# Zero products in TensorE's planned waits, a pattern's spread moved to GpSimd's queue, later keys, and new due times

## The chip, the cores and the metric

The kernel runs on one core of a Trainium2 chip. The metric is device time in microseconds of that core; the time before is the median of three runs. A profile is one more execution, recorded instruction by instruction. The engines are TensorE (PE; its weight loads are listed as PEld), VectorE (DVE), ScalarE (ACT), GpSimd (POOL) and SyncE (SP), each with its own queue, which it works through in order.

## The reference

Four sequences, eight heads, 768 positions, 64 dimensions per head. Attention looks at six chunks of 32 keys per query, chosen by an upper bound on the chunk's scores, and its result goes through a gated feed-forward network with 512 inputs and 1536 hidden units:

```
k_min, k_max = min, max of k over each chunk of 32 keys
ub     = sum(max(q * k_min, q * k_max))            # per query and chunk
ub     = ub where the chunk is not behind the query, else -1e9
sel    = the 6 chunks with the largest ub
scores = q @ k.T / 8, -1e9 outside sel and behind the query
x      = softmax(scores) @ v                       # heads side by side: 3072 x 512
out    = (sigmoid(x @ w_gate) * (x @ w_val)) @ w_out
```

## The kernel before

The work is cut into nine stages: the first sequence in three (128, 256 and 384 queries), each further sequence in two halves of 384. A stage has three parts. `prep` brings keys and queries with the head dimension on partitions (`kTp`, `qT` in the first three stages, transposes on VectorE later), takes minimum and maximum per chunk (`kxn`, `kcat`), multiplies the bounds out (`m_ub`, L969), compares with the sixth largest and puts the result as 25 more rows under the queries in `headQ` (L997). Stage zero has so few chunks that nothing is selected; it has a guard instead (`first_guard`, `m_ub` at L936). `attn` makes scores (`big_sc` or `m_sc`, L1046) against `headK`, whose 25 rows at partition 64 hold the patterns that turn the 25 rows of `headQ` into a mask, then the exponential (`at`, L1051), the diagonal's mask on GpSimd (L1057), the product with the values (`m_pv`, L1071), the division (`xnat`) and the transpose (`m_xtp`, L1096). `ffn` makes `m_g` and `m_v` (L1125), the gate (L1134), `hglu` (L1136) and `m_o` (L1146), and stores it.

Nothing is written in the order in which it runs. Each piece is a task in `Plan`, with a priority (a due time plus entries of the table `NUDGE`), one or several engines with a duration each, the keys that it reads and writes, and its tiles. `order` puts the tasks on the engines with those durations, and the program is emitted in the order of the planned starts. So the table and the constants decide the order on each engine; on the chip the engines wait for each other by semaphores alone. Tasks on the lanes `Q0` and `Q2` are empty: they stand for a transfer's landing in the plan and emit nothing. `WLAND` holds the planned landings of the nine thirds of weights (`weight_tasks`: w0 to w5 are `wg` and `wv` in turn, w6 to w8 are `wo`, all issued by GpSimd), and `LOADS` those of the first sequence's keys, queries, values and pattern spreads on SP's and ScalarE's queues.

A spread (`_spread`, L646) copies the 25 rows of a pattern, made by `_pattern` on GpSimd for one head, to the other heads by a DMA. The spread for the first half (`p00`) goes by SP's queue. The loads of the next sequences' keys and queries (`_blocks`, L661) go by SP's queue too, and so do the stores of `out` (L1161). `fill` (L581) emits products of zeros into a bank of PSUM; the plan calls it only ahead of TensorE's first task.

Of the kernel before, what the change touches and what calls it, by code (L numbers as in the profile page):

```python
# [8 lines left out]
F32 = mybir.dt.float32  # L9
F16 = mybir.dt.float16  # L10
# [12 lines left out]
    "#c.0": 0.4, "#c.1": -7.8, "wst0": -58.5, "#wst0.0": -1.1, "w0": -26.5, "#w0.0": 2.5, "#c.2": -0.1, "wst1": -42.4,  # L23
    "#wst1.0": 77.9, "w1": 59.5, "#w1.0": -28.8, "#c.3": -8.7, "#c.4": -30.2, "v": 61.3, "#v.0": 12.6, "wst2": 4.3,
    "#wst2.0": -73.1, "w2": -9.6, "#w2.0": 2.9, "#c.5": 6.6, "#c.6": 6.2, "wst3": -12.3, "#wst3.0": -1.3, "w3": 31.2,
    "wst4": 0.2, "#wst4.0": 0.2, "w4": -1.7, "#w4.0": -30.1, "wst5": 20.7, "#wst5.0": 62.1, "w5": 1.3, "#w5.0": -16.3,
    "wst6": 2.6, "#wst6.0": 63.7, "w6": 34.0, "#w6.0": 26.2, "wst7": -36.4, "#wst7.0": -22.5, "w7": -9.8,
    "wst8": -28.7, "#wst8.0": 184.1, "w8": -13.6, "#w8.0": 15.0, "#c.7": 28.2, "#c.8": 65.6, "kch": 94.9,
    "#kch.0": 10.3, "is": -163.2, "qch": 120.2, "#qch.0": 3.5, "vn": -29.4, "#vn.0": -16.8, "#is.1": -44.3,
    "#vn.1": -1.6, "#kch.1": -9.0, "#qch.1": 11.7, "#kch.2": -19.3, "#qch.2": 5.6, "#is.2": 25.2, "#vn.2": -8.5,  # L30
    "#c.9": 7.3, "#vn.3": -9.2, "#v.1": -1.9, "#v.2": 0.6, "#v.3": 9.4, "kTp0": -37.9, "prep:0": -5.0,
    "#kTp:0.0": -4.5, "kxn0": -126.7, "#kxn:0.0": -41.0, "#kxn:0.1": -0.4, "#kc:0.0": 45.4, "hk0": 1.5,
    "#hk:0.0": 3.0, "#hk:0.1": 16.0, "#hk:0.2": 6.0, "#hk:0.3": 0.8, "qT0": 3.8, "#qT:0.0": 4.6, "Qc0": -121.7,
    "#Qc:0.0": 7.2, "#Qc:0.1": -14.0, "#Qc:0.2": -5.2, "#Qc:0.3": -1.9, "ubp0": -30.8, "#ubp:0.0": -23.3,
    "#ubp:0.1": 19.4, "#c.10": -30.9, "#c.11": -6.7, "gT0": -4.3, "#gT:0.0": -23.1, "#gT:0.1": 6.5, "#c.12": -9.9,
    "Ap0": 10.2, "#Ap:0.0": -3.8, "#Ap:0.1": -11.3, "#c.13": -18.6, "v0": 6.8, "load:0": 54.9, "#v:0.0": 11.2,
    "#v:0.1": -90.7, "sc0": -12.2, "attn:0": -38.0, "#sc:0.0": 1.4, "at0": -27.1, "#at:0.0": -7.4, "#at:0.1": -37.4,
    "pv0": -22.8, "#pv:0.0": 63.4, "#pv:0.1": -10.0, "#pv:0.2": -4.6, "#pv:0.3": 23.2, "xn0": -12.6, "#xn:0.0": 33.2,
    "xtp0": -31.4, "#xtp:0.0": -7.3, "xT0": 59.7, "#xT:0.0": 56.1, "#sc:0.1": 25.2, "#at:0.2": 37.5, "#at:0.3": 10.0,
    "#pv:0.4": -20.9, "#pv:0.5": -1.7, "#pv:0.6": -62.7, "#pv:0.7": 25.8, "#xn:0.1": 30.1, "#xtp:0.1": -0.4,  # L40
    "#xT:0.1": 4.2, "#kch.3": 69.9, "#qch.3": -9.0, "#kch.4": 25.8, "#qch.4": 3.2, "#kch.5": -3.5, "#qch.5": -0.9,
    "#c.15": 2.7, "#vn.4": -3.2, "#v.4": -23.4, "#vn.5": 23.4, "#v.5": 72.9, "#vn.6": 26.6, "#v.6": -22.5, "gv0": 0.4,
    "ffn:0": 2.1, "#gv:0.0": -31.3, "#gv:0.1": -14.7, "#gv:0.2": 17.1, "#gv:0.3": -12.2, "#gv:0.4": 45.7,
    "#gv:0.5": 1.8, "#gate:0.0": -21.5, "hglu0": 21.2, "#hglu:0.0": 60.4, "#gv:0.6": -2.4, "#gv:0.7": 46.8,
    "#gv:0.8": 3.1, "#gv:0.10": -11.2, "#gate:0.1": -22.7, "#hglu:0.1": -27.8, "#gv:0.12": -16.4, "#gv:0.13": -20.6,
    "#gv:0.14": -7.9, "#gv:0.15": 5.9, "#gv:0.16": 28.2, "#gv:0.17": 20.7, "#gate:0.2": 7.7, "#hglu:0.2": -0.4,
    "#gv:0.18": 20.0, "#gv:0.19": 1.6, "#gv:0.20": -8.1, "#gv:0.21": 10.7, "#gv:0.22": 41.9, "#gv:0.23": 8.8,
    "#gate:0.3": -5.2, "#hglu:0.3": 12.5, "o0": 0.6, "#o:0.0": 20.6, "#o:0.1": -8.9, "#o:0.2": 17.4, "#o:0.3": 56.4,
    "#o:0.4": 13.4, "#o:0.5": -24.0, "#osb:0.0": -16.7, "out0": 17.0, "kTp1": 6.5, "prep:1": -1.7, "#kTp:1.0": -2.1,
    "kxn1": 37.4, "#kxn:1.0": -46.3, "#kxn:1.1": 7.9, "#kTp:1.1": 11.8, "#kxn:1.2": 27.8, "kc1": 0.1, "#kc:1.0": 24.9,  # L50
    "hk1": 41.1, "#hk:1.0": -36.9, "#hk:1.1": 18.5, "#hk:1.2": -11.6, "#hk:1.3": 30.2, "qT1": -33.9, "#qT:1.0": -31.0,
    "Qc1": 103.7, "#Qc:1.0": 26.5, "#Qc:1.1": -10.1, "#Qc:1.2": -10.3, "#Qc:1.3": 12.8, "#qT:1.1": 15.6,
    "#Qc:1.4": 5.7, "#Qc:1.5": -21.6, "#Qc:1.6": -18.7, "#Qc:1.7": -21.2, "#hq:1.0": -10.7, "#hq:1.1": -0.6,
    "ub1": -2.1, "ubq1": -27.3, "#ubq:1.0": -21.1, "#ubq:1.1": 47.9, "mx81": -5.0, "#mx8:1.0": -48.4, "Ap1": 4.8,
    "#Ap:1.0": 15.8, "apT1": -41.3, "#apT:1.0": 20.4, "mq1": 2.4, "#mq:1.0": 3.4, "#mq:1.1": -18.2, "#mq:1.2": 25.8,
    "#mq:1.3": 25.9, "#ub:1.1": 27.0, "#ubq:1.2": 9.4, "#ubq:1.3": 2.8, "#mx8:1.1": 26.0, "#Ap:1.1": 26.7,
    "#apT:1.1": 4.0, "#mq:1.5": 24.9, "#mq:1.6": 2.4, "#mq:1.7": -39.3, "sc1": 1.4, "attn:1": -238.2, "#sc:1.0": -6.4,
# [1173 lines left out]
```

## Time and profile before

| | us |
|---|---|
| median of three runs | 304.28 (304.17 to 304.63) |
| the profiled execution | 305.13 |
| its span, first to last instruction | 303.3 |
| TensorE busy | 285.6 |
| VectorE busy | 213.6 |
| ScalarE busy | 196.4 |
| GpSimd busy | 111.2 |

The mean granted clock of TensorE is 0.960 of full. The page cuts the span into 40 slices and gives the busy tenths of each engine and the granted clock; groups of instructions follow by line and tile, with their count, busy time and mean, and the idle time ahead of them with what ended it. In rows in order of time the first number is the start, the second the duration (of all instructions of the row), then the engine, the line, the operation and its tiles. A wait is put down to what came last. A matmul's end is modelled, so the pace of a row of matmuls is better read from the start of the next one.

### The profile page before, as it was taken

The page shows a single profiled execution, that of the slowest core. Times are in us where ns is not written, and L with a number is a line of the kernel's source. Part 1 is how long each engine was busy: PE and PEld are TensorE (multiplying, and loading weights), DVE is VectorE, ACT ScalarE, POOL GpSimd, SP SyncE. Part 2 cuts the span into 40 slices and gives each one's busy share as a digit, 9 for nine tenths or more (in the row PEclk, how much of TensorE's full clock was granted, in tenths as well). Part 3 has the DMA queues.
Part 4 walks back from the last instruction along what each step waited for, and adds up shares of the span by engine and source line. Part 5 has one row for each costly group of instructions (what it writes and reads, how often), then busy time and mean ns, then how long its engine had stood idle before and what let it go on. Part 6 is the DMA issues. An engine that isn't in the chain of part 4 may idle for free.

```text
span 303.3 us, 6733 instructions
## 1 busy us (share of the span) xinstructions
PE 285.6 (94%) x2594; PEld 183.1 (60%) x2594; DVE 213.6 (70%) x585; ACT 196.4 (65%) x292; POOL 111.2 (37%) x176
## 2 busy tenths in 40 slices
PE   7466999999999999999999999999999999999994
PEld 3344995776566556665656566676656666655551
DVE  3677289899999899989998995898667234221322
ACT  2685789699496589578965667599644825622322
POOL 7944711286667243117941242058312001200000
PEclk9657599999999999999999999999999999999999
DMA  7999999999999570511970100018000000120102
GB/s 153 267 212 268 230 173 106 169 159 158 167 163 176 108 161 4 87 19 40 182 93 1 50 21 3 0 37 85 5 2 35 37 0 2 37 104 0 71 0 104
DMA packets 110004, 27.98 MB, mean 92 GB/s; under 512 B 100207, under 2 KB 105365, under 8 KB 109973
## 3 DMA queue, kind: packets, MB, share of 16 engines
q1 hardware_dynamic: 81669, 19.43, 31.7%
q0 software_dynamic: 26592, 7.47, 24.5%
q10 hardware_dynamic: 1712, 0.66, 0.9%
q8 instruction: 20, 0.33, 0.4%
q14 instruction: 11, 0.09, 0.1%
HBM read 28.31 MB, written 6.29 MB: 114 GB/s over the span
## 4 chain that ended last, share of the span: by engine, by line
PE 81%; DMA 7%; DVE 5%; POOL 2%; ACT 1%; issue 1%; SPq 0%; POOLq 0%; DVEq 0%; ACTq 0%
PE m_o L1146 18%; PE m_v L1125 17%; PE m_g L1125 16%; PE big_sc L1046 12%; PE m_pv L1071 7%; DMA ld_v<-in_v_dram 6%; PE big_gv L1125 5%; PE m_ub L969 4%; PE m_xtp L1096 2%; DMA ld_qb<-in_q_dram 1%; DVE Qcat L909 1%; DVE kxn L809 1%; DVE kT_kT L878 1%; DVE hglu L1136 0%; DVE Qcat L765 0%
## 5 line engine op out<-in xcount | busy, mean ns | idle before, releaser
L1051 ACT ACTIVATE at<-big_sc 128x896 f16<-128x896 f32 (+3 forms) x96 | 84.0, 908 | 21.1 <-PE big_sc L1046 19.1
L1146 PE MATMUL m_o<-wo,hglu 128*128 128x512 f16 x288 | 73.6, 379 | 0.0
L1125 PE MATMUL m_g<-xT,wg 128*128 128x384 f16 (+2 forms) x384 | 69.0, 312 | 1.4 <-ACT xT L1100 1.4
L1125 PE MATMUL m_v<-xT,wv 128*128 128x384 f16 (+2 forms) x384 | 69.2, 310 | 0.2 <-DVE hglu L1136 0.2
L1136 DVE SCALAR_TENSOR_TENSOR hglu<-gate,m_v 128x384 f16<-128x384 f16 (+1 forms) x88 | 45.5, 531 | 29.7 <-PE m_v L1125 23.9
L1057 POOL TENSOR_SCALAR_AFFINE_SELECT at<-at 128x384 f16<-128x384 f16 (+2 forms) x66 | 34.8, 531 | 85.7 <-ACT at L1051 81.8
L1134 ACT ACTIVATE gate<-m_g 128x384 f16<-128x384 f32 (+1 forms) x88 | 39.9, 475 | 29.5 <-PE m_g L1125 18.4
L1125 PEld LDWEIGHTS <-wg 128*128 128x128 f16 x432 | 41.0, 101 | 23.5 <-issue 2.8
L1125 PEld LDWEIGHTS <-wv 128*128 128x128 f16 x432 | 40.2, 100 | 22.9 <-issue 1.9
L1046 PE MATMUL big_sc<-headQ,headK 89*128 89x128 f16 (+2 forms) x472 | 51.0, 246 | 2.7 <-ACT headQ L997 1.8
L1046 PEld LDWEIGHTS <-headK 89*128 89x128 f16 x472 | 34.1, 99 | 15.6 <-issue 4.8
L1146 PEld LDWEIGHTS <-hglu 128*128 128x128 f16 x288 | 25.6, 97 | 21.6 <-issue 1.2
L1071 PEld LDWEIGHTS <-at 128*128 128x128 f16 x672 | 30.5, 100 | 12.3 <-issue 3.1
L1071 PE MATMUL m_pv<-v,at 128*128 128x65 f16 x672 | 34.9, 196 | 0.0
L997 POOL COPY headQ<-apT 25x384 f16<-25x384 f16 (+1 forms) x33 | 16.2, 491 | 36.4 <-DVE apT L993 35.3
L909 DVE STREAM_TRANSPOSE Qcat<-ld_qb 64x768 f32<-64x768 f32 x24 | 23.1, 967 | 0.4
L776 POOL CAST headQ<-Qcat 64x1536 f16<-64x1536 f32 (+1 forms) x11 | 15.6, 1420 | 20.9 <-ACT Qcat L761 10.9
L1136 DVE SCALAR_TENSOR_TENSOR hglu<-gate,big_gv 128x384 f16<-128x384 f16 x12 | 6.5, 552 | 18.2 <-ACT gate L1134 7.8
L1083 DVE TENSOR_TENSOR xnat<-m_pv,rz 128x384 f16<-128x384 f32 (+1 forms) x34 | 18.2, 534 | 1.2
L1153 ACT ACTIVATE osb<-m_o 128x512 f32<-128x512 f32 x16 | 9.5, 597 | 12.5 <-PE m_o L1146 12.2
L1134 ACT ACTIVATE gate<-big_gv 128x384 f16<-128x384 f32 x12 | 5.8, 490 | 17.9 <-PE big_gv L1125 17.3
L680 POOL DMA_DIRECT2D v<-in_v_dram x18 | 16.3, 922 | 0.5 <-PE m_pv L1071 0.5
(109 smaller groups left out, 301.0 us busy)
## 6 DMA issues: line engine op xcount, KB each, us to landing
out_dram<-osb SPq DMA_DIRECT2D x24, 256.0 KB, 2.0
ld_kb<-in_k_dram SPq DMA_DIRECT2D x24, 192.0 KB, 3.5
ld_qb<-in_q_dram SPq DMA_DIRECT2D x24, 192.0 KB, 4.0
v<-in_v_dram POOLq DMA_DIRECT2D x21, 128.0 KB, 7.3
ld_k<-in_k_dram SPq DMA_DIRECT2D x6, 256.0 KB, 14.2
wg<-in_moe_w_gate_dram POOLq DMA_DIRECT2D x3, 512.0 KB, 15.1
wv<-in_moe_w_val_dram POOLq DMA_DIRECT2D x3, 512.0 KB, 15.4
wo<-in_moe_w_out_dram POOLq DMA_DIRECT2D x3, 512.0 KB, 30.2
```

The source lines that it names most:

```text
L680: nc.gpsimd.dma_start(dst[:, :, i, :], v[b, :, r0 + 128 * i:r0 + 128 * i + 128].rearrange("h p d -> p h d"))
L909: nc.vector.transpose(tl(qd, [128, H, HS])[0:64, h:h + 2].rearrange("p a (c t) -> p a c t", t=CH), tl(("ld", "qb", b, u))[64 * e:64 * e + ...
L997: copy(tl(("headQ", s), [89, H, st.n], F16)[64:89, h, :], tl(apT)[32 * i:32 * i + 25, :])
L1046: nc.tensor.matmul(ps[:, 128 * o:128 * (o + m)], (hk if s else firstK)[0:rows, h, jl:jl + 128], (tl(("headQ", s)) if s else first)[0:rows, ...
L1051: add(at(x + 0.03 * t + 0.01), [("ACT", 0.19 + w * 0.815e-3, lambda sc=sc, a=a, w=w: nc.scalar.activation(tl(a, [128, 1024], F16)[:, 0:w], ...
L1057: nc.gpsimd.affine_select(out=dg, in_=dg, compare_op=ALU.is_ge, fill=0.0, base=0, pattern=[[0, nd], [1, 128]], channel_multiplier=-1)
L1071: nc.tensor.matmul(pvp[:, ib - q0, h % HP, :], tl(a)[:, 128 * o:128 * o + 128], head_v(b, jb // HB)[:, h, jb % HB, :], start=(jb == 0), st ...
L1083: nc.vector.tensor_tensor(dst, pvp[:, :, :, 0:64], r.to_broadcast([128, nb, HP, 64]), ALU.mult)
L1125: nc.tensor.matmul(ps(i)[:, n * (fb - f0):n * (fb - f0 + 1)], w16[:, c, 128 * fb:128 * fb + 128], tl(("xT", s, c // 2))[:, c % 2, :], star ...
L1134: add(at(x) - EV, [("ACT", 0.18 + 0.81 * el, lambda gate=gate, ps=ps: nc.scalar.activation(tl(gate, [128, G * n], F16), ps(0), AF.Tanh, sc ...
L1136: add(at(x) - EV, [("DVE", 0.15 + 1.04 * el, lambda gate=gate, hg=hg, ps=ps: nc.vector.scalar_tensor_tensor(tl(hg, [128, G * n], F16), tl( ...
L1146: nc.tensor.matmul(tl(o, [128, 512]), tl(("hglu", s, fc // G))[:, c0:c0 + 128], wo16[:, fc, :], start=(fc == 0), stop=(fc == NFB - 1))
```

## The change

Four things are changed together.

A task on TensorE can carry a `room`: a function that gives a part of the PSUM tile that the task will write. Where the plan leaves TensorE idle by more than 0.25 us ahead of such a task, between 5.5 and 36 us of the plan, products of zeros are emitted into that tile, as many as take 95% of the planned wait at the full clock. The transposes of keys and queries, `m_ub`, the guard's transpose, the scores, `m_pv`, `m_xtp`, and `m_g` and `m_v` carry one. The task that follows overwrites the tile. `m_ub` of stage zero takes a whole bank for it.

The spread `p00` is issued by GpSimd after w2, ahead of w3, and is gone from SP's list.

The keys and queries of the second sequence are planned behind the landing of w8, not w7.

`NUDGE` is new in nearly all of its some 1,800 entries, and `WLAND` and `LOADS` have new numbers.

```diff
-                    out.append((t - fills * each - 0.1, len(out), None, fills))
+                    out.append((t - fills * each - 0.1, len(out), None, (fills,)))
+            room = self.tasks[i][5]
+            if eng == "PE" and room and self.warm[0] < t < self.warm[1]:
+                tl, since = self.tasks[i][3][0], max(free.get("PE", 0.0), slot_time(i))
+                since = max([since] + [till + LATENCY[e] for e, till in used.get(tl, {}).items() if e != "PE"])
+                if t - since > 0.25:
+                    out.append((t, len(out), None, (t - since - 0.05, room, tl not in given)))
...
-    plan = Plan({**SB, **PS}, PS, cold_until=7.0, filler=("m", 0.22, None))
+    plan = Plan({**SB, **PS}, PS, cold_until=7.0, filler=("m", 0.22, None), warm=(5.5, 36.0))
...
-    def fill(n):
-        ps = tl(("m", "fill"), [128, 512])
+    def fill(n, ps=None):
+        if ps is None:
+            ps = tl(("m", "fill"), [128, 512])
         for _ in range(n):
-            nc.tensor.matmul(ps, zeros[:, 0:128], zeros, start=True, stop=True)
+            nc.tensor.matmul(ps, zeros[:, 0:128], zeros[:, 0:ps.shape[-1]], start=True, stop=True)
...
         add(-89, [("POOL", 1.6, lambda: _pattern(0))], r=["id16"], w=["pat0"])
+        add(-79, [("POOL", 0.95, lambda: _spread(nc.gpsimd, 0, 0))], r=["pat0"], w=[("ps", 0), "issue"])
+        add(-79, [("Q0", 0.8, None)], r=[("ps", 0)], w=[("pl", 0), "hkc00", "lane0"])
         for n in range(3, 9):
-            weight_tasks(n, -80 + n, ["pat0"])
+            weight_tasks(n, -78 + n, ["pat0"])
...
-                            r=[("w", 7)] if b == 1 else [], w=[(n, b, u, j), "lane"], tiles=[("ld", n, b, u)])
+                            r=[("w", 8)] if b == 1 else [], w=[(n, b, u, j), "lane"], tiles=[("ld", n, b, u)])
...
-    WLAND = [9.0, 14.3, 18.5, 22.5, 28.8, 33.8, 37.0, 40.2, 43.3]
+    WLAND = [9.4, 14.8, 19.0, 23.0, 27.2, 31.8, 35.1, 38.1, 41.3]
...
         for i, o in plan.order():
-            if i is None:
-                fill(o)
+            if i is None and len(o) > 1:
+                ps = o[1](o[2])
+                fill(int(0.95 * o[0] / (ps.shape[-1] / 2400 + 0.003)), ps)
+            elif i is None:
+                fill(*o)
```

In `LOADS` the entry `("SP", "p00", 17.6)` is gone, the first eight landings move by up to 0.6 us, `v11` by 0.2, and the last three `v` by -2.0.

42 lines of the change are left out of this document (23 added, 19 removed), and 595 rows, old and new, of tables (LOADS, NUDGE).

## The prediction

> **What bounds the kernel now.** I read the page's busy lines and slices first, then the same quantities in stretches of 3.41 us, then TensorE's waits, then the first 45 us engine by engine.
>
> ```profile
> span 303.3 us, 6733 instructions
> PE 285.6 (94%) x2594; PEld 183.1 (60%) x2594; DVE 213.6 (70%) x585; ACT 196.4 (65%) x292; POOL 111.2 (37%) x176
> PEclk9657599999999999999999999999999999999999
> ```
>
> TensorE is busy for 285.6 of 303.3 us, and the clock row is below full only in the first six slices and the last. So what the change can win lies ahead of about 37 us; behind it these are all of TensorE's waits, 1.9 us together:
>
> ```profile
> PE m_g L1125 <- ACT xT L1100: 0.6, 1, 0.6
> PE m_xtp L1096 <- DVE xnat L1083: 0.5, 1, 0.5
> PE big_sc L1046 <- DMA ld_qb<-in_q_dram: 0.4, 1, 0.4
> PE m_ub L969 <- ACT Qcat L761: 0.2, 1, 0.2
> PE m_v L1125 <- DVE hglu L1136: 0.2, 1, 0.2
> ```
>
> The start in stretches (stretch, its length, then busy us of PE, PEld, DVE, ACT, POOL; then the granted clock):
>
> ```profile
> 5.72:9.14 3.42, 0.95 (x7) 0.46 (x5) 2.87 (x8) 1.72 (x3) 3.15 (x7) 1.00 1.19 201
> 9.14:12.55 3.41, 0.95 (x11) 0.87 (x12) 1.88 (x6) 2.20 (x4) 3.41 (x6) 0.50 1.15 277
> 22.79:26.20 3.41, 3.41 (x33) 2.40 (x31) 1.85 (x5) 1.15 (x2) 2.47 (x3) 0.50 1.17 261
> 26.20:29.61 3.41, 1.62 (x22) 1.03 (x21) 3.13 (x23) 2.10 (x5) 0.79 (x2) 1.00 1.14 273
> 29.61:33.03 3.42, 2.90 (x32) 2.60 (x31) 0.97 (x3) 3.18 (x6) 2.36 (x6) 0.50 1.19 250
> 33.03:36.44 3.41, 3.41 (x37) 3.22 (x35) 1.20 (x5) 2.25 (x4) 2.52 (x6) 0.50 1.21 227
> 36.44:39.85 3.41, 3.41 (x58) 3.38 (x56) 2.15 (x7) 2.09 (x5) 2.13 (x3) 1.00 1.42 207
> 60.00:150.00 90.00, 88.72 (x887) 56.03 (x886) 85.11 (x220) 71.04 (x96) 48.00 (x62) 1.00 0.82 117
> ```
>
> The clock changes only at these edges, and each stretch shows the verdict on the one before it: 28% busy (0.95 of 3.42) took the clock away, 47% (1.62) took it away again, 85% (2.90) did not bring it back, 100% (3.41) did. Between 47% and 85% nothing is shown of keeping it.
>
> **The prices and the present chain.** TensorE, then GpSimd with the way to landing (us) of the first `wv` and of the third `wo`, then ScalarE, in order of time:
>
> ```profile
> 1.29 4.02 PE L581 MATMUL m_fill<-zeros 128*128 128x512 f16 x9 [1.29 <-DVE zeros L586]
> 6.71 0.66 PE L800 MATMUL m_qT<-ident,ld_q 128*128 128x128 f32 x4 [0.69 <-DMA ld_q<-in_q_dram]
> 10.44 0.37 PE L936 MATMUL m_ub<-kcat,first 128*128 128x4 f16 x8 [3.07 <-DVE headK L849]
> 16.77 0.42 PE L1071 MATMUL m_pv<-v,at 128*128 128x65 f16 x4
> 24.08 1.04 PE L1125 MATMUL m_g<-xT,wg 128*128 128x128 f16 x8
> 26.52 0.64 PE L969 MATMUL m_ub<-Qcat,kcat 128*32 128x256 f32 x8
> 28.95 0.71 PE L1046 MATMUL big_sc<-headQ,headK 89*128 89x128 f16 x8 [1.79 <-ACT headQ L997]
> 38.52 0.83 PE L1125 MATMUL m_g<-xT,wg 128*128 128x128 f16 x12
> 39.64 0.39 PE L1096 MATMUL m_xtp<-ident,xnat 128*128 128x128 f16 x4
> 46.27 1.46 PE L1146 MATMUL m_o<-wo,hglu 128*128 128x512 f16 x6
> ```
>
> ```profile
> 2.73 0.77 POOL L746 DMA_DIRECT2D wv<-in_moe_w_val_dram  x1
> wv<-in_moe_w_val_dram POOLq DMA_DIRECT2D x1, 512.0 KB, 12.9
> 10.04 2.25 POOL L748 DMA_DIRECT2D wo<-in_moe_w_out_dram  x3
> wo<-in_moe_w_out_dram POOLq DMA_DIRECT2D x1, 512.0 KB, 33.7
> 12.24 0.49 POOL L593 MEMSET headK<- 25x384 f16 x1
> 16.06 0.65 POOL L1057 TENSOR_SCALAR_AFFINE_SELECT at<-at 128x512 f16<-128x512 f16 x1 [0.28 <-ACT at L1051]
> 19.87 0.89 POOL L717 DMA_DIRECT2D v<-in_v_dram  x1 [1.62 <-DMA wg<-in_moe_w_gate_dram]
> ```
>
> ```profile
> 27.85 0.63 ACT L730 CAST v<-ld_v 128x512 f16<-128x512 f32 x1 [0.73 <-DMA ld_v<-in_v_dram]
> 29.43 1.30 ACT L1051 ACTIVATE at<-big_sc 128x640 f16<-128x640 f32 x2
> 35.12 1.51 ACT L1051 ACTIVATE at<-big_sc 128x640 f16<-128x640 f32 x2 [0.53 <-PE big_sc L1046]
> ```
>
> VectorE (the first and the last of six rows that follow each other without a wait) and SP:
>
> ```profile
> 27.65 0.41 DVE L972 STREAM_TRANSPOSE ubq<-m_ub 128x256 f32<-128x256 f32 x1
> ...
> 29.52 0.45 DVE L993 STREAM_TRANSPOSE apT<-Ap 128x256 f16<-128x256 f16 x1
> ```
>
> ```profile
> 7.87 0.95 SPq L646 DMA_DIRECT2D headK<-headK  x1
> 50.39 2.68 SPq L1161 DMA_DIRECT2D out_dram<-osb  x1
> ```
>
> A product of zeros of 512 columns costs 0.43 us at half clock (4.02/9, less the last one's tail) and 0.215 at full clock, as `m_o` does (1.29 us of pace for six). A product of 128 columns costs 0.104 at half clock (eight before the next start, 0.83 us) and 0.056 at full (twelve in 0.67). The mark in the chain that I follow is the first `big_sc` of stage one at 28.95.
>
> **Part 1: the first pattern's spread goes from SP's to GpSimd's queue.** SP loses one issue (0.95 us, and its wait for the pattern), so the values behind it, which land at 27.85 and hold ScalarE for 0.7 us before `headQ`, are issued earlier; in the changed order GpSimd casts them, and this wait leaves the chain. GpSimd gains one issue, between 0.75 (2.25/3) and 0.89 us. What stands behind matters more. The built program gives GpSimd's loads eight semaphores in turn, and a ninth load waits until the first has landed:
>
> ```
> before  wo (third)   waits DMASW0   (landed by the first wg)
> before  v16_10       waits DMASW1, DMASW2, DMASW3
> after   wo (second)  waits DMASW0
> after   wo (third)   waits DMASW1   (landed by the first wv)
> ```
>
> That such a wait stops GpSimd is the row at 19.87: 1.62 us idle until a `wg` landed. The first `wv` lands at 2.73 + 12.9 = 15.6. So in the changed kernel the third `wo` is issued at 15.6 to 16.4, and behind it in order stand `pen3`, the second pattern and three memsets. Before, that work (12.24 to 15.78, where the mask's idle time of 0.28 begins; 3.5 us) lay ahead of the mask; without the two `Ap` memsets, 0.7 us, which are now later, it is 2.8 us. The first mask of stage zero then starts at 19.2, not 16.06, and ends at 19.8; the second ends at 20.5. The load itself loses nothing: its queue is busy with the earlier ones. I call this the hold. It is excluded only if the first `wv` lands by 12.4, and its row leaves 3 us to that.
>
> **Part 2: the products of zeros.** The changed order has 8 at the start, then 2 before `m_qT`, 11 before `m_ub`, 3 before the stage-one `qT`, 2 and 4 (260 columns) before the two groups of `m_pv`, 5 (128) before `xtp`, 6 (384) before `m_g`, 10 before the first `big_sc`. They have a fixed count; only those in a real wait are free. The 2 + 11 are: 2.4 us at full clock between 7.1 and 9.6, and `m_ub` needs `first` at 10.4. The 5.72 to 9.14 stretch becomes about 85% busy. The next has 0.4 us of zeros, `m_ub` and one transpose, 1.3 of 3.41 or 39%, below the 47% that lost the clock: half clock from 12.55. The 3 then cost 1.3 us instead of 0.65, hidden behind the hold. From about 16.8 to 19.8 TensorE waits for the mask with 2 products of 0.11 us, since the count knows no hold: 15.96 to 19.37 is 25 to 30% busy, and the clock is down (or stays down) at 19.37.
>
> Then, at half clock: `m_pv` 0.25 (its 0.42 less the last product's tail), four zeros 0.87, `m_pv` 0.25, five zeros 0.5, `xtp` 0.25, `qT` 0.85: 22.8. The stretch to 22.79 is 87% busy, just above the 85% that did not suffice. I take it that the clock comes back there (100% is the other end, treated as a rival). Then `xtp` 0.2, six zeros of 384 columns 0.97, 36 products of 128 columns 2.0: 26.0; two `m_ub` 0.55 each, the first done at 26.6. From there VectorE's six steps take 2.3 us (27.65 to 29.97) and the copy to `headQ` under 0.5 (ScalarE's cast ends at 28.48, `big_sc` starts at 28.95); the second half's transpose and cut, now between them, add 0.6: 3.4 to 3.5. The first `big_sc` comes at 30.1, 1.1 us later than 28.95. The ten zeros (2.2 us) end before it.
>
> What comes next runs at full clock. Before, from 28.95 to the second `xtp` at 39.64 there are 10.7 us, of which 0.5 is waiting and 3.1 half-clock loss (6.2 us busy up to 36.44): 7.1 us of work. That is the upper end of the gain, 3.6. The lower is ScalarE: eight exponentials at 0.65 to 0.70, a copy and a `gate` make 6.4 us where now 29.43 to 36.63 are 7.2, and with the 3.0 us behind them 9.4: a gain of 1.3. I take 2.2, between them, because `m_g`, `m_v` and transposes stand among the `big_sc` and fill part of ScalarE's time.
>
> **Parts 3 and 4: keys of sequence two behind the last weight; new due times.** The planner's landing of a weight is an empty task, so no wait is added to a queue: only orders move. On SP the first store of `out` no longer stands between the keys and the queries; the store held SP (50.39, 2.68 us) and TensorE then waited 0.4 us for `ld_qb`. I count -0.4; the other end is 0. For the remaining order I count nothing: the work is the same, the waits are 1.9 us, so the gain is at most 1.5 more; as the loss I take at most 1.1, the two largest waits once more, most likely where DVE has only 4.9 us free in the 90 us from 60 to 150.
>
> **Sum.** +1.1 - 2.2 - 0.4 = -1.5. The profiled execution took 305.13 us (span 303.3), the median of the three runs is 304.28; a profiled 303.6 answers to 302.8 as a median. Its own ends: +1.1 - 3.6 - 0.4 gives 301.4, +1.1 - 1.3 gives 304.1.
>
> **The rivals.** *Half clock until 26.2 (slower).* 87% was not enough, as 85% was not. Six zeros take 1.9 us, up to 25.0; 11 of the 36 products run at 0.104, 25 at 0.056: 27.6; `m_ub`, then 3.4 us: `big_sc` at 31.6, +2.65. With a later gain of 1.3 to 2.2 and the queries' wait unchanged this is 304.7 to 305.6, centre 305.2. It decides once the delay exceeds what the later full clock returns, 1.3 to 3.6 us.
>
> *The clock is never lost at 19.37.* Then the chain from the mask is 0.45 of zeros, `m_pv`, `xtp` at 21.2, `qT`, `xtp` at 21.7, zeros 0.97, products 2.0, `m_ub`: `big_sc` at 28.7, -0.25, in sum -2.85: 301.4. Against it is the row of 26.20, where 47% lost it. The Trainium skill, "TensorE: Matmul & The Clock Gate", section "HAM oscillation — how this bites in real kernels", gives as its rule that idle gaps over about 3.4 us bring half clock; the wait of 3.0 us is shorter, and by that rule this rival's 301.4 holds. The trace's stretch from 26.20, with no wait over 1.8 us, does not agree.
>
> *No hold.* If the first `wv` landed in time, the mask stays at 16.06, `big_sc` comes near 26.2, and -2.75 - 2.2 - 0.4 = -5.3; but the last third of `wo` lands at 45.2 (issued 11.5, 33.7 on the way) and the last four of stage zero's `m_o`, 1.7 us behind 46.27 - 5.3, would wait some 2.5 us for it: -2.8, 301.5.
>
> *DVE takes it back.* It is busy 85.11 of 90 us from 60 to 150; a TensorE that arrives earlier waits there: 304.2.
>
> **Numbers.** Forecast 0.35, half clock until 26.2 0.33, clock never lost 0.11, no hold 0.09, DVE 0.12. About 0.2% (0.6 us) is what a measurement can tell from no change. Faster by more: most of the first, the third and fourth, 0.51; within: parts of the forecast and the slow case and most of DVE's, 0.15; slower 0.34. The range, 300.6 to 305.6, leaves out the far ends of the no-hold and slow cases.
>
> **What would show it.** The third `wo` issue waiting for `wv`; the first mask near 19; the clock's edges at 12.55, 19.37 and 22.79; the first `big_sc` near 30; full clock from 29.6 to 36.4; no wait for `ld_qb`. It is wrong if the mask stays at 16, if the edges fall elsewhere, or if a new wait of over 1 us appears on TensorE behind 60 us.

## The result and the profile after

The changed kernel takes 307.10 us as a median (306.55 to 307.34), the kernel before on the same chip 304.23. The ratio is 1.009, with a 95% interval of 1.0073 to 1.0106: slower by 2.9 us, where 302.8 us had been predicted.

The profiled execution of the changed kernel took 306.55 us, 1.4 more than the profiled execution of before. The rest of the 2.9 us lies in which executions were profiled. That of before, at 305.13, was 0.9 slower than the median of its kernel. That of after is the lowest of its kernel: the others have spans of 305.3 to 305.6 us at a mean clock of 0.983 instead of 0.989. As an estimate, that difference of 0.006 over 305 us is 3.7 us more at half clock, about one more stretch of 3.41 us.

The head of the page of after:

```profile
span 304.8 us, 6804 instructions
PE 288.4 (95%) x2636; PEld 181.9 (60%) x2636; DVE 209.5 (69%) x578; ACT 198.1 (65%) x294; POOL 116.7 (38%) x182
PEclk9978999999999999999999999999999999999999
```

The clock row has become better: 9, 9, 7, 8 in place of 9, 6, 5, 7, 5, 9. TensorE lost less time to half clock and the kernel still became slower. The rows of GpSimd of after, in order of time, show where it began (start, duration, instruction, and in brackets the idle time before it and what ended it):

```profile
11.19 1.52 POOL L754 DMA_DIRECT2D wo<-in_moe_w_out_dram  x2
15.52 0.74 POOL L754 DMA_DIRECT2D wo<-in_moe_w_out_dram  x1 [2.81 <-DMA wv<-in_moe_w_val_dram]
...
19.22 1.24 POOL L1064 TENSOR_SCALAR_AFFINE_SELECT at<-at 128x512 f16<-128x512 f16 x2
...
25.07 0.87 POOL L723 DMA_DIRECT2D v<-in_v_dram  x1 [2.47 <-DMA wv<-in_moe_w_val_dram]
25.93 0.44 POOL L643 MEMSET Ap<- 128x384 f16 x1
...
26.85 0.43 POOL L643 MEMSET Ap<- 128x384 f16 x1
27.21 1.04 POOL L782 CAST headQ<-Qcat 64x1024 f16<-64x1024 f32 x1
```

The hold is there: the third `wo` waits 2.81 us for the first `wv`, and the masks start at 19.22. There is a second one that the prediction did not have. The third load of the values waits 2.47 us for the last `wv`, and the two `Ap` memsets and the cast of `headQ` stand behind it. TensorE of after:

```profile
19.92 0.40 PE L1078 MATMUL m_pv<-v,at 128*128 128x65 f16 x4 [5.03 <-POOL at L1064]
23.02 2.13 PE L585 MATMUL m_g<-zeros 128*128 128x384 f16 x6
27.37 1.07 PE L976 MATMUL m_ub<-Qcat,kcat 128*32 128x256 f32 x16
31.37 0.71 PE L1053 MATMUL big_sc<-headQ,headK 89*128 89x128 f16 x8 [0.66 <-DVE headQ L1004]
40.22 0.40 PE L1104 MATMUL m_xtp<-ident,xnat 128*128 128x128 f16 x4
47.55 2.75 PE L1156 MATMUL m_o<-wo,hglu 128*128 128x512 f16 x12
```

TensorE waits 5.03 us for the mask and reaches the first `big_sc` at 31.37, 2.42 us later than before (28.95). The first `m_o` comes 1.28 us later (47.55 against 46.27), so 1.14 us are won back in between. Behind that some 0.2 us are lost again. What the wait of 0.66 us for `headQ` goes back to is a row of VectorE, which waited for TensorE's late `m_ub`, when the second `Ap` memset had been done at 27.28:

```profile
28.08 0.45 DVE L979 STREAM_TRANSPOSE ubq<-m_ub 128x256 f32<-128x256 f32 x1 [2.98 <-PE m_ub L976]
```

The granted clock falls to half at 18.79 and is full again from 25.62. The stretches of 3.41 us that fit these edges (columns as in the prediction):

```profile
5.14:8.55 3.41, 3.41 (x20) 1.77 (x19) 2.88 (x9) 2.05 (x3) 2.84 (x7) 1.00 1.18 226
8.55:11.96 3.41, 1.96 (x18) 1.03 (x16) 2.55 (x7) 2.87 (x6) 3.41 (x6) 1.00 1.16 283
11.96:15.38 3.42, 2.04 (x19) 1.50 (x18) 3.36 (x6) 2.95 (x6) 0.75 (x2) 1.00 1.19 241
15.38:18.79 3.41, 0.00 (x0) 0.00 (x0) 0.01 (x1) 1.38 (x3) 2.90 (x9) 1.00 1.22 212
18.79:22.20 3.41, 2.28 (x21) 2.02 (x22) 1.21 (x5) 0.00 (x0) 2.95 (x6) 0.50 1.17 232
22.20:25.62 3.42, 3.42 (x19) 2.35 (x18) 2.62 (x8) 2.50 (x5) 0.95 (x2) 0.50 1.14 283
25.62:29.03 3.41, 3.41 (x51) 2.37 (x50) 0.81 (x4) 1.91 (x3) 3.19 (x6) 1.00 1.16 274
```

Behind the stretches that were 57% and 60% busy the clock stayed full, behind the empty one it fell at 18.79, behind the one of 67% at half clock it stayed half, and behind the one of 100% it came back at 25.62. TensorE's waits behind 60 us are these:

```profile
PE m_pv L1078 <- ACT osb L1163: 0.7, 1, 0.7
PE m_xtp L1104 <- DVE xnat L1091: 0.4, 1, 0.4
PE m_ub L976 <- ACT Qcat L924: 0.2, 1, 0.2
PE big_sc L1053 <- ACT at L1058: 0.2, 1, 0.2
```

The wait for `ld_qb` has gone (0.4), and one for `osb` is new (0.7).

### The profile page after: what moved, and what is told of

Its sections match the earlier page's. It is cut to its first block, busy times and chain, and to the rows that moved or that the text cites. A ratio compares the mean times of both kernels' runs of the same rounds, so it can differ in the third digit from the quotient of the medians.

```text
span 304.8 us, 6804 instructions
## 1 busy us (share of the span) xinstructions
PE 288.4 (95%) x2636; PEld 181.9 (60%) x2636; DVE 209.5 (69%) x578; ACT 198.1 (65%) x294; POOL 116.7 (38%) x182
## 4 chain that ended last, share of the span: by engine, by line
PE 76%; ACT 6%; DMA 6%; DVE 5%; POOL 3%; issue 2%; SPq 0%; DVEq 0%; POOLq 0%; ACTq 0%
PE m_o L1156 17%; PE m_g L1134 15%; PE m_v L1134 15%; PE big_sc L1053 10%; PE m_pv L1078 7%; PE big_gv L1134 5%; DMA wg<-in_moe_w_gate_dram 5%; PE m_ub L976 3%; PE m_xtp L1104 1%; ACT Qcat L924 1%; ACT Qcat L767 1%; DVE Qcat L915 1%; DMA ld_kb<-in_k_dram 1%; POOL headK L904 1%; ACT gate L1144 1%
## 5 line engine op out<-in xcount | busy, mean ns | idle before, releaser
L1058 ACT ACTIVATE at<-big_sc 128x1024 f16<-128x1024 f32 (+3 forms) x96 | 83.5, 908 | 17.1 <-PE big_sc L1053 12.8
L1156 PE MATMUL m_o<-wo,hglu 128*128 128x512 f16 x288 | 72.8, 379 | 0.0
L1064 POOL TENSOR_SCALAR_AFFINE_SELECT at<-at 128x384 f16<-128x384 f16 (+2 forms) x66 | 33.9, 520 | 81.3 <-ACT at L1058 77.7
L1134 PEld LDWEIGHTS <-wg 128*128 128x128 f16 x432 | 39.6, 98 | 23.7 <-issue 2.5
L1134 PEld LDWEIGHTS <-wv 128*128 128x128 f16 x432 | 39.4, 98 | 22.7 <-issue 1.9
L1053 PE MATMUL big_sc<-headQ,headK 89*128 89x128 f16 (+2 forms) x472 | 49.7, 240 | 1.5 <-ACT at L1058 0.8
L1053 PEld LDWEIGHTS <-headK 89*128 89x128 f16 x472 | 32.9, 97 | 13.8 <-issue 3.6
L782 POOL CAST headQ<-Qcat 64x1536 f16<-64x1536 f32 (+1 forms) x14 | 20.7, 1482 | 21.5 <-DVE Qcat L915 11.7
L1163 ACT ACTIVATE osb<-m_o 128x512 f32<-128x512 f32 x18 | 10.7, 597 | 18.7 <-PE m_o L1156 16.2
L1091 DVE TENSOR_TENSOR xnat<-m_pv,rz 128x384 f16<-128x384 f32 (+1 forms) x34 | 18.1, 534 | 1.2
L1089 DVE RECIPROCAL rz<-m_pv 128x6 f32<-128x6 f32 (+1 forms) x34 | 6.3, 186 | 18.1 <-PE m_pv L1078 17.7
```

The lines of the kernel that those rows point to most:

```text
L782: copy(tl(("headQ", s), [89, H, st.n], F16)[0:64, h0:h0 + 4, :], tl(("Qcat", s))[0:64, h0:h0 + 4])
L1053: nc.tensor.matmul(ps[:, 128 * o:128 * (o + m)], (hk if s else firstK)[0:rows, h, jl:jl + 128], (tl(("headQ", s)) if s else first)[0:rows, ...
L1058: add(at(x + 0.03 * t + 0.01), [("ACT", 0.19 + w * 0.815e-3, lambda sc=sc, a=a, w=w: nc.scalar.activation(tl(a, [128, 1024], F16)[:, 0:w], ...
L1064: nc.gpsimd.affine_select(out=dg, in_=dg, compare_op=ALU.is_ge, fill=0.0, base=0, pattern=[[0, nd], [1, 128]], channel_multiplier=-1)
L1091: nc.vector.tensor_tensor(dst, pvp[:, :, :, 0:64], r.to_broadcast([128, nb, HP, 64]), ALU.mult)
L1134: nc.tensor.matmul(ps(i)[:, n * (fb - f0):n * (fb - f0 + 1)], w16[:, c, 128 * fb:128 * fb + 128], tl(("xT", s, c // 2))[:, c % 2, :], star ...
```

## The experiments

The theory at the start was that the hold makes the loss, by the late mask and the half clock behind it. The rivals were that the products of zeros make it by delaying TensorE, and that the new due times do. After the first four runs the second hold was added to the theory. In the diffs `...` stands for lines left out, and the comments behind `#` are put in for reading. All kernels compute the whole result; those without zeros leave out only products of zeros that are overwritten. The first `big_sc` and the first `m_o` are starts in the profiled execution, the median and the ratio come from all executions. The first line's median is the range over the chips on which it was measured again beside the others. The profiled execution lies near the median of its kernel in most lines, but it was 1.3 us above it for the spread on GpSimd in the order of before and 1.0 above it for the third `wo` behind the masks, so the starts in these two lines are late; it was 0.9 us below it for values moved without zeros. That of before lies 0.7 to 1.0 above.

| kernel | first `big_sc` | first `m_o` | span | median | ratio to before, interval |
|---|---|---|---|---|---|
| before | 28.95 | 46.27 | 303.3 | 304.1 to 304.4 | 1 |
| changed | 31.37 | 47.55 | 304.8 | 307.10 | 1.0090 (1.0073 to 1.0106) |
| changed, no zeros | 30.64 | 47.35 | 304.6 | 306.68 | 1.0082 (1.0055 to 1.0110) |
| changed, third `wo` behind the masks | 30.18 | 48.44 | 305.7 | 306.44 | 1.0068 (1.0048 to 1.0088) |
| changed, the wait filled with zeros | 30.57 | 47.3 | 304.6 | 306.27 | 1.0059 (1.0035 to 1.0083) |
| changed, spread back on SP | 28.86 | 47.0 | 304.2 | 305.52 | 1.0038 (1.0022 to 1.0053) |
| changed, `wo` and `Ap` moved | 27.88 | 45.95 | 303.4 | 305.63 | 1.0044 (1.0028 to 1.0060) |
| changed, `wo`, `Ap` and values moved | 26.05 | 44.01 | 303.9 | 306.20 | 1.0069 (1.0036 to 1.0101) |
| before, spread on GpSimd | 32.36 | 49.24 | 306.3 | 306.94 | 1.0086 (1.0052 to 1.0120) |
| before, zeros | 27.55 | 44.81 | 301.8 | 303.82 | 0.9978 (0.9963 to 0.9993) |
| before, zeros and ten more | 28.35 | 45.0 | 302.0 | 304.36 | 1.0001 (0.9983 to 1.0019) |
| before, values moved | 27.76 | 44.72 | 301.7 | 304.50 | 0.9998 (0.9971 to 1.0024) |
| before, zeros, values moved | 25.14 | 42.95 | 302.5 | 304.55 | 1.0005 (0.9979 to 1.0030) |
| before, zeros, values moved, queries first | 26.40 | 43.83 | 301.9 | 303.78 | 0.9988 (0.9974 to 1.0003) |

### Part 1 alone, and everything but part 1

In the order of before, only the spread is taken from SP's place and issued by GpSimd behind the pattern:

```diff
...
+        spread = steps.pop(key.index("hkc00"))
+        steps.insert(key.index("pat0") + 1, spread)     # issued by nc.gpsimd
```

> The kernel before with the first pattern's spread alone moved from SP's queue to GpSimd's, behind the pattern; order and due times of all else unchanged, no zeros. Hold theory: the third `wo` waits until 15.5, the first mask starts at 19.2 to 19.9 instead of 16.06, `big_sc` at 30.5 to 32, and the time is 306 to 308. Zeros theory and order theory: the spread costs nothing that is seen, 303.5 to 304.5.

Measured: 306.94 us, 1.0086. GpSimd and TensorE:

```profile
15.64 0.74 POOL L750 DMA_DIRECT2D wo<-in_moe_w_out_dram  x1 [2.94 <-DMA wv<-in_moe_w_val_dram]
19.73 0.65 POOL L1059 TENSOR_SCALAR_AFFINE_SELECT at<-at 128x512 f16<-128x512 f16 x1
```

```profile
32.36 0.71 PE L1048 MATMUL big_sc<-headQ,headK 89*128 89x128 f16 x8 [0.51 <-ACT headQ L999]
```

The one moved DMA reproduces the hold and, with 2.6 of 2.9 us, nearly the whole size of the loss. The first mask is 3.7 us later than before, `big_sc` 3.4 and the end of the profiled execution 3.0. In this order the `Ap` memsets stand ahead of the masks, so the second hold plays no part. The added issue (0.83 us) also moves every load behind it: the last `wv` is issued at 10.46, not 9.31, as in the changed kernel. How much of the 2.6 us that is, this run can't tell.

The reverse, the changed kernel with the spread issued from SP again:

```diff
-        add(-79, [("POOL", 0.95, lambda: _spread(nc.gpsimd, 0, 0))], r=["pat0"], w=[("ps", 0), "issue"])
+        add(-79, [("POOL", 0.95, lambda: _spread(nc.sync, 0, 0))], r=["pat0"], w=[("ps", 0), "issue"])
...
+        spread = steps.pop(key.index(("ps", 0)))
...
+        steps.insert(key.index(("vn", 1, 1, 0)), spread)     # ahead of v11 on SP's queue
```

> The changed kernel with part 1 alone undone: the first pattern's spread is issued from SP's queue again; zeros, keys of sequence two and due times stay as changed. If GpSimd's queue is the whole cause (two holds: the third wo behind the first wv, and the Ap memsets behind the values' load that waits for the last wv), GpSimd waits nowhere ahead of the first mask, the mask starts at 15.5 to 16.5, the first big_sc of stage one at 27.5 to 28.5, and the time is that of the kernel before with zeros, 303.8, give or take 0.6. If the new due times carry a part of the loss, the mask is just as early, but the time stays at 305.3 or more and waits of over 1 us appear behind 60 us. If the zeros and the due times together gain more than before with zeros alone, it is below 303.2.

Measured: 305.52 us, 1.0038. The hold is gone (masks at 15.26), and so are 1.6 of the 2.9 us. The rest stays, against the theory in its first form, though without the waits of over 1 us behind 60 us that the rival named; the longest there is 0.7, for `osb`. GpSimd and TensorE:

```profile
23.93 0.88 POOL L725 DMA_DIRECT2D v<-in_v_dram  x1 [3.59 <-DMA wv<-in_moe_w_val_dram]
24.80 0.44 POOL L645 MEMSET Ap<- 128x384 f16 x1
25.71 0.43 POOL L645 MEMSET Ap<- 128x384 f16 x1
26.07 1.04 POOL L784 CAST headQ<-Qcat 64x1024 f16<-64x1024 f32 x1
```

```profile
28.86 0.71 PE L1055 MATMUL big_sc<-headQ,headK 89*128 89x128 f16 x8 [2.82 <-DVE headQ L1006]
```

The second hold is here too, so it belongs not to the spread but to the new order, which puts the `Ap` memsets behind the third load of the values. Against the order of before with zeros (next but one) `big_sc` is 1.31 us later, and the way from there to the first `m_o` is 0.8 us longer (18.1 against 17.26). The spans differ by 2.4 us (304.2 against 301.8), so only about 0.2 us of this loss lies behind the first `m_o`: the new order costs at the start, not in the later stages.

### The zeros

The changed kernel without them:

```diff
             if i is None and len(o) > 1:
-                ps = o[1](o[2])
-                fill(int(0.95 * o[0] / (ps.shape[-1] / 2400 + 0.003)), ps)
+                continue
```

> The changed kernel without the products of zeros in planned waits; the eight at the start stay, the order of all else is the same. Hold theory: the masks stay at 19.2, TensorE loses the some 3.5 us of zeros between 20 and 25 but nothing brings the clock back before stage one's scores, so the first `big_sc` comes at 29.5 to 31.5 at half clock and the time is 306 to 308. Zeros theory: the time falls to 304.5 or below. Order theory: 306 to 308 too, with the same waits behind 60 us as with zeros.

Measured: 306.68 us; the intervals overlap, so in the changed kernel the zeros are worth nothing that can be told. Without them `big_sc` waits 3.79 us for `headQ` instead of 0.66 and comes at 30.64: TensorE is early and idle instead of late and busy.

The order of before, with the zeros and nothing else of the change:

> The kernel before, its order, due times and queues unchanged, with the products of zeros in its own planned waits between 5.5 and 36 us: some 50 more matmuls, nothing else. Hold theory: without the hold the clock stays up from 5.7 us but for at most one or two stretches, the first `big_sc` of stage one comes at 26 to 28.5 instead of 28.95, and the time is 301 to 303. Zeros theory: the zeros run late and the time is 304.5 or above. Order theory: 303 or below.

Measured: 303.82 us, 0.9978 with an interval below 1. This part alone is a small gain, about 0.7 us. The clock is full to about 28 us and `big_sc` is 1.4 us earlier, 27.55. But it waits:

```profile
27.55 2.84 PE L1054 MATMUL big_sc<-headQ,headK 89*128 89x128 f16 x16 [2.35 <-ACT headQ L1005]
```

and GpSimd and VectorE show for what:

```profile
24.78 0.88 POOL L724 DMA_DIRECT2D v<-in_v_dram  x1 [4.53 <-DMA wv<-in_moe_w_val_dram]
25.65 0.63 POOL L737 CAST v<-ld_v 128x512 f16<-128x512 f32 x1
26.20 1.05 POOL L783 CAST headQ<-Qcat 64x1024 f16<-64x1024 f32 x1
```

```profile
25.61 1.85 DVE L998 TENSOR_TENSOR Ap<-ubq,mx 128x192 f16<-128x192 f32 x1
```

The load of values that waits for the last `wv` holds the cast of `headQ` in the kernel before as well. There TensorE, at half clock, was about as late.

Ten more zeros in that wait of 2.35 us:

```diff
+                if ps.shape[-1] == 512 and count == 6:
+                    count += 10
```

> The kernel before with the planned zeros, and ten more products of 512 columns (2.15 us at full clock) in the wait of 2.35 us before stage one's first big_sc, where the clock went to half for two stretches from about 28 to 35. If the half clock there sets the end, the clock stays full, the second xtp and the first m_o come 1.3 to 2.2 us earlier, and the time is 301.6 to 302.5. If ScalarE's exponentials bound that stretch, the clock stays full but the time is 303.3 to 304.0. If the zeros run past headQ and delay big_sc, it is 304 or more.

Measured: 304.36 us. The clock is full to 31.24 instead of 27.75 and at half for one stretch instead of two, and no gain can be told. The time is that of the third expectation, but not by its cause: `big_sc` came at 28.35, later than 27.55, and waited 0.90 us for `headQ` behind the last zero, so the zeros did not delay it. What held it was ScalarE's cast of values, 3.40 us idle for a load that landed at 27.25, ahead of its copy to `headQ`. Without the ten zeros this cast started at 26.44. So such a landing lies 0.8 us apart in two executions of nearly equal kernels, and single starts of one profile are no surer than that.

### The two holds, one and then both

> The changed kernel with one issue moved: GpSimd issues the third `wo` behind the two masks of stage zero, no longer ahead of them. Hold theory (the wait for the first `wv` delays the masks and lets the clock fall): the first mask starts near 16.3 instead of 19.2, the first `big_sc` of stage one comes at 27 to 28.5 instead of 31.4, the half clock at 18.6 to 25.4 is gone or shorter, and the time falls by 3 to 4 us, to 303 to 304. Zeros theory (the products of zeros delay TensorE by themselves): the mask is early, yet the first `big_sc` stays above 30 and the time above 306. Order theory (the new due times cost in the later stages): `big_sc` is early, but the time stays at 306 to 307.

The edit moves one load in the emitted order:

```diff
+        late = next(x for x in steps if x[0] is not None and plan.kinds[x[0]][-1] == "#wst8.0")     # third wo
+        steps.remove(late)
...
+        steps.insert(mask + 1, late)          # behind the second mask of stage zero
```

Measured: 306.44 us. GpSimd and VectorE:

```profile
15.68 1.24 POOL L1064 TENSOR_SCALAR_AFFINE_SELECT at<-at 128x512 f16<-128x512 f16 x2
...
25.38 0.87 POOL L723 DMA_DIRECT2D v<-in_v_dram  x1 [3.52 <-DMA wv<-in_moe_w_val_dram]
26.24 0.44 POOL L643 MEMSET Ap<- 128x384 f16 x1
```

```profile
27.62 1.16 DVE L997 TENSOR_TENSOR Ap<-ubq,mx 128x192 f16<-128x192 f32 x1 [3.69 <-POOL Ap L643]
```

The masks are 3.5 us earlier and `big_sc` 1.2: the second hold has taken the first one's place, VectorE waiting 3.69 us for a memset. The signs named for the zeros theory (an early mask, `big_sc` above 30, a time above 306) are all there, but not its cause: TensorE had done its zeros and waited 5.03 us for `headQ`.

The wait for the masks filled with zeros, both holds left:

```diff
+                if ps.shape[-1] == 260 and count == 2:
+                    count += 40
```

> The changed kernel with 42 instead of 2 products of zeros (260 columns) in TensorE's wait of 5.0 us for the first mask, 4.5 us at full clock; both holds stay. If the half clock after the first hold is what costs, the clock stays full to 28 at least, the first big_sc comes at 28.7 to 29.2 and the time is 304 to 305. If the second hold is the cost (Ap memsets at 25.9 and 26.9, headQ behind them), big_sc comes no earlier than 30.0 to 30.4 although the clock is full, and the time is 305.4 to 306.5.

Measured: 306.27 us, and

```profile
30.57 0.71 PE L1053 MATMUL big_sc<-headQ,headK 89*128 89x128 f16 x8 [1.61 <-DVE headQ L1004]
```

The clock was half once, from 11.3 to 14.8, and full from there to 31.8. The time is what the second hold gives, and `big_sc` is 0.2 us above its upper end, far from the half clock's 28.7 to 29.2. By the ratios the clock behind the first hold is worth 0.9 us (1.0090 to 1.0059), and the intervals overlap, so most of the loss is not the clock's. In the changed kernel itself TensorE's work at half clock ends last (0.66 us of waiting); with the clock kept the second hold does.

Both moved, with the spread still on GpSimd:

```diff
+        steps.insert(mask + 1, late)
...
+            steps.insert(mask + 1 + i, early)     # the two Ap memsets, ahead of it
```

> The changed kernel, spread still on GpSimd's queue, but with two pieces of GpSimd's order moved: the third wo load stands behind the two masks, and right behind it the two Ap memsets stand ahead of the loads of sequence two's values. If the two holds in GpSimd's queue are the cause and not the queue that issues the spread, the masks start at 15.7, the Ap memsets at 17 to 19.5, the first big_sc at 27.5 to 28.5 (it was 30.18 with the first hold alone removed), and the time is 303.2 to 304.4. If the second hold costs nothing (the rival: only the mask's lateness counts), the time stays at the 306.4 of the run with the first hold alone removed. If the due times cost, 305.3 or more with an early big_sc.

Measured: 305.63 us, and `big_sc` at 27.88 as expected. With the spread still on GpSimd the time is that of the run with the spread back on SP (305.52), which keeps the second hold. So a good part of its price is what stands behind the waits. Not all of it: there the third load of the values starts at 23.93, here at 25.35, as the last `wv` is issued 1.2 us later. And with the second hold in both, the run with the third `wo` moved takes 0.9 us longer than that with the spread on SP (306.44 against 305.52; the intervals just overlap). Still the time is 1.2 us above the upper end expected, in the range given for costly due times. From `big_sc` to the first `m_o` this order takes 18.07 us, that of before with zeros 17.26, both with two stretches at half clock; there the new due times cost something of their own. And the two casts, of values at 26.22 and of `headQ` at 26.78 to 27.82, still behind the third load of the values, now meet VectorE:

```profile
26.30 1.57 DVE L1000 TENSOR_SCALAR Ap<-mx 128x8 f16<-128x8 f32 x1
```

### The third wait, and what is under it

In the order of before, the third load of values goes behind the copies to `headQ`, and the two casts of stage one's values behind the work they stood ahead of:

```diff
...
+        steps.insert(last, steps.pop(late))              # third load of v16_10
...
+        steps.insert(half + 1, casts[0])                 # behind headQ's first half
...
+        steps.insert(exps[1] + 1, casts[1])              # behind the second exponential
```

> The kernel before with the planned zeros, and three steps of the values moved behind work they stood ahead of: the third load of sequence two's values (GpSimd waits 4.5 us in it for the last wv, with the cast of headQ and the copies to headQ behind it) goes behind stage one's last copy to headQ, and the two casts of stage one's values go behind the copies to headQ of its first half (GpSimd) and behind the second exponential (ScalarE, which waited 2.7 us in its cast for that load). If this wait of GpSimd's queue paces the start in every kernel here, the cast of headQ starts near 21 instead of 26.2, VectorE's stretched step (1.85 us beside that cast) becomes short, the first big_sc comes at 25.0 to 26.0 instead of 27.55 and the time is 301.5 to 302.8. If ScalarE's exponentials or the landing of the values set the end of that stretch, big_sc is early but the time stays at 303.3 to 304.

Measured: 304.55 us, no gain. `big_sc` is at 25.14 as expected, VectorE's step takes 0.56 instead of 1.85 us, the clock is full from 7 us to the last stretch, and the first `m_o` comes at 42.95, 3.3 us ahead of before and 1.9 ahead of before with zeros. At the `m_ub` near 72 us (72.14) it is 1.0 us ahead of before (73.17) and 0.4 behind before with zeros (71.73). VectorE and TensorE in between:

```profile
58.20 0.97 DVE L918 STREAM_TRANSPOSE Qcat<-ld_qb 64x768 f32<-64x768 f32 x1 [2.49 <-DMA ld_qb<-in_q_dram]
```

```profile
61.53 0.49 PE L1081 MATMUL m_pv<-v,at 128*128 128x65 f16 x10 [1.19 <-POOL at L1067]
```

The queries of sequence two have not landed, and VectorE's steps behind them, `headQ` and the mask among them, wait.

> The changed kernel, spread still on GpSimd's queue, with every wait in that queue moved off the way to stage one: third wo behind the masks, Ap memsets right behind them, third load of sequence two's values and the casts of stage one's values moved as in the run of before. If only waits in GpSimd's queue made the changed kernel slow, the first big_sc comes at 24.8 to 26.0 and the time is that of before with the same moves, within 0.5. If the new due times cost something of their own (the run with the spread back on SP was 1.7 above before with zeros), it stays 1 us or more above it, with the waits of m_pv for osb (0.7) and of big_kqT for Qcat (0.5) on TensorE.

The changed kernel with the moves of both kinds: 306.20 us, `big_sc` at 26.05, and the same floor a little earlier, at the keys:

```profile
55.11 0.98 DVE L886 STREAM_TRANSPOSE kT_kT<-ld_kb 128x768 f32<-128x768 f32 x1 [2.86 <-DMA ld_kb<-in_k_dram]
```

With all three waits moved out of the way the changed order is still 1.6 us above before with the same moves, of which 0.9 lie ahead of `big_sc` (26.05 against 25.14). That part belongs to the order, or to the spread's place, since here it is still on GpSimd's queue; the pair with the spread on SP in both kernels gave 1.7.

> The kernel before without any zeros, with the same three steps of the values moved. If the wait in GpSimd's queue set the first big_sc in the kernel before too, it comes 0.5 to 1.5 earlier than 28.95 and the time is 303.0 to 303.9. If half clock bounds the start there, so that TensorE's own work ends last, big_sc stays within 0.4 of 28.95 and the time within 0.5 of before.

Measured: 304.50 us with `big_sc` at 27.76, 1.2 earlier. By the ratio, 0.9998 over six executions, no gain can be told. The profiled execution is the fastest of its kernel (303.59); in it VectorE did not wait for the queries, and the lead over the profiled execution of before was kept to the end (303.59 against 305.13). Why the median won nothing isn't settled.

Last, the store that stands on SP's queue between the keys and these queries goes behind them, as in the changed kernel:

```diff
+        store = steps.pop(place(("out", 0, 0)))
...
+        steps.insert(query + 1, store)
```

> The run of before with zeros and the values' three steps moved, and one step more: on SP's queue the first store of out (3.1 us in the queue there) goes behind the four loads of sequence two's first queries, as the changed kernel has it. In that run the first m_o came 1.9 us earlier than with zeros alone, and all of it was lost when VectorE waited 2.5 us for these queries until 58.2. If the landing of sequence two's loads is the floor on which a faster start runs up, VectorE waits under 0.5 us for them, TensorE's lead of 1.9 us survives past 70 us, and the time is 302.0 to 303.0. If the transfers of the start themselves are the limit (their engines are over 90% busy to 47 us), the queries land no more than 1 us earlier and the time stays at 303.8 to 304.6.

Measured: 303.78 us, 0.9988, between the two expectations and next to the second, with the queries transposed 1.35 us earlier. VectorE:

```profile
56.85 0.97 DVE L918 STREAM_TRANSPOSE Qcat<-ld_qb 64x768 f32<-64x768 f32 x1 [0.26 <-issue]
...
64.48 0.98 DVE L887 STREAM_TRANSPOSE kT_kT<-ld_kb 128x768 f32<-128x768 f32 x1 [0.55 <-DMA ld_kb<-in_k_dram]
```

The wait for the queries is gone, and the next one, for the next keys, has come. TensorE's lead over before with zeros is 0.98 us at the first `m_o` and 0.3 at the `m_ub` near 71 us. The lowest ratio of all remains that of the kernel with the least changed, before with zeros, 0.7 us under before; the interval of this last run overlaps it.

## Why the prediction was wrong

It said 302.8 us, from +1.1 - 2.2 - 0.4 on the profiled time of before. At the prediction's own marks the profiled execution of after shows +2.42 at the first `big_sc`, -1.84 from there to the second `xtp` (8.85 us, 31.37 to 40.22, against 10.69) and +0.9 from there to TensorE's end: +1.5. That is 3 us of the miss; the other 1.4 is how far the two profiled executions lie from their medians.

- **The hold** was right in each of its steps: the third `wo` at 15.52 (15.6 to 16.4), the first mask at 19.22 (19.2), by the wait for the first `wv`. By the prediction's own rival without a hold (301.5) it was worth 1.3 us; undoing it in the changed kernel gave back 1.6, and in the order of before the moved spread alone costs 2.6. But without the hold 305.52 was measured, not 301.5, so the larger errors are elsewhere. Not counted was that all of GpSimd's loads behind the spread are issued about 1.2 us later.
- **The clock at 12.55** was wrong: it was not lost there. The edges lie at 5.14, 8.55 and so on, 0.6 us from where before had them, and the stretches held 57% and 60% of work instead of the 39% expected in the one before 12.55. It did not matter, since the work there waits for the mask anyway. In the run with the wait filled, which is the same program up to that wait, the clock was lost, from 11.34 to 14.75.
- **The first step that failed** is "I take it that the clock comes back there", at 22.79. With the other edges the stretch behind the mask was 18.79 to 22.20, of which TensorE's wait took the first 1.13 us; it was 67% busy, not 87%, and the clock came back only at 25.62. Until then 15 products of zeros and the transposes between them ran at half speed, and `m_ub` was first done near 28.0, not 26.6. The chain behind it took 3.3 us (28.08 to 31.37) against the 3.4 to 3.5 assumed. So `big_sc` came at 31.37, not 30.1, which is the slow rival's 31.6. That is 1.3 us of the miss, and the clock is not all of it: with the clock kept by more zeros `big_sc` still came at 30.57, held by the `Ap` memsets, and the time was 306.27.
- **The second step that failed**, and by the ratios the larger, is "For the remaining order I count nothing", with the -0.4 of part 3. From the second `xtp` to the end the profile shows +0.9 in place of -0.4. By the ratios, from before with zeros (0.9978) to the changed kernel with the spread on SP (1.0038), the keys and due times together cost about 1.8 us, above the prediction's bound of 1.1. In the two profiled executions 2.2 of the 2.4 us between them lie ahead of the first `m_o`, by the second hold among others, not in the stages behind 60 us where the prediction looked for the loss.
- **The later full clock** was about right: 2.2 was taken, between 1.3 and 3.6, and 1.84 came, for nearly the same products (8 more of `m_v`, 4 transposes fewer). Two `big_sc` rows wait for `at` there (0.53 and 0.16), as the lower end of ScalarE's exponentials had it. 0.7 of the 1.84 us are lost again up to the first `m_o`, 0.46 of them in a wait of a transpose for `Qcat` at 47.09.
- **Parts 3 and 4** in detail: the wait for `ld_qb` did go, and the wait for `osb` (0.7) came. How the 1.8 us divides between the keys and the table wasn't tried.
- **"The two `Ap` memsets, 0.7 us, which are now later"** were counted as time saved ahead of the mask. They are the second hold. In the changed kernel itself its cost is covered by TensorE's lateness; it is the price that appears as soon as the first hold is mended.
- **The slow rival** had the place and the mechanism. Its 304.7 to 305.6 is a median; against before's profiled execution it is 305.6 to 306.5, and 306.55 was measured there. That this fits so well is partly luck: the rival has no second hold and no loss by the order, and the median, 307.10, lies 1.5 us above its range.
- **DVE takes it back** did not happen in the changed kernel, which is not early. In two kernels that were early VectorE did take time back: not by its own work, but by its wait for the keys and queries of sequence two (2.49 and 2.86 us).

Taken one after the other, the steps from before to the changed kernel are: zeros -0.7, due times and keys +1.8, spread on GpSimd +1.6 (1.0038 to 1.0090), together +2.7. They add up by their making, so the sum is no proof, and the split depends on the order in which the parts are taken: in the order of before and without zeros the spread is worth 2.6. The intervals of the single ratios are about 1 us wide, so each term is good to some 0.6 us.

On the clock, the Trainium skill, "TensorE: Matmul & The Clock Gate", section "HAM oscillation — how this bites in real kernels", has idle gaps over about 3.4 us as what brings half clock. The wait of 5.03 us in after agrees, and so does the empty stretch at 15.38. This section's rule does not cover the stretch of before that was 47% busy without such a gap. Nor does the busy share of a stretch, by which the prediction judged, decide it. These stretches are from the kernel before with ten more zeros, the one with the spread on GpSimd, and the changed one with the third `wo` behind the masks:

```profile
27.82:31.24 3.42, 2.12 (x27) 1.64 (x27) 0.73 (x2) 3.27 (x7) 1.32 (x4) 1.00 1.15 273
32.12:35.54 3.42, 2.42 (x29) 1.81 (x28) 2.44 (x14) 3.27 (x7) 1.49 (x4) 1.00 1.35 220
13.95:17.36 3.41, 1.85 (x23) 1.41 (x23) 2.27 (x6) 2.77 (x5) 3.18 (x7) 1.00 1.22 204
```

Behind the first, 62% busy, and the second, 71%, the clock fell to half; behind the third, 54%, it stayed full. At half clock a stretch with 3.14 us busy (28.71 to 32.12, spread on GpSimd) brought it back, and one with 3.16 (31.01 to 34.43, third `wo` behind the masks) did not. What decides between 47% and 100% stays open here.

## What to carry to other kernels

When a DMA issue is moved into a queue, count the waits and the delay that it hands to every later issue there, and list what stands behind each of them: removing the first hold exposed a second, that a third, and that the landing of the next loads. A gain at the start is worth its size only if the next fixed landing has room for it; look for the next transfer that the early engine will meet before counting the gain. Where a verdict depends on the granted clock in one stretch, price the case that the stretch begins elsewhere, since its edges are not fixed to the program.

## What was not expected of the hardware

The clock's edges lie on a grid of 3.41 us, which lies differently against the program in each execution: 5.72, 9.14 and so on in before, 5.14, 8.55 in after. The same work falls into other stretches and can get another verdict.

VectorE's short steps stretch when GpSimd casts. The comparison into `Ap` takes 0.36 us alone and took 1.85 us in before with zeros (25.61 to 27.46), while GpSimd's casts of values and of `headQ` ran from 25.65 to 27.25. In the changed kernel with two moves the step after it, 0.18 us alone, took 1.57 us (26.30 to 27.87) beside the casts from 26.22 to 27.82. With the cast of `headQ` moved to 21 us the comparison took 0.56. The Trainium skill, "SBUF — State Buffer", section "🔬 SBUF: two separate sides", says that VectorE, in a 2-port mode or with two inputs in SBUF, and GpSimd share a port pair as an exclusive lock, so that the later one waits until the other's instruction is done. That both steps end 0.05 to 0.21 us behind a cast agrees with it; in the first case VectorE's step is recorded as starting 0.04 us ahead of the casts, and whether the second step runs in such a mode the trace doesn't show.
